# One 224 KB coefficient load, B_C_im, moved from ScalarE's DMA queue to SyncE's

## The chip, the cores and the metric

The kernel runs on one core of a Trainium2 chip. The metric is the device time in microseconds (us) of one execution. A load or a store is issued by an instruction on SyncE's queue (SPq in the profile) or on ScalarE's queue (ACTq), in the order in which the program put the instructions there; the DMA engines then move the data while the issuing engine goes on.

## The reference, cut to what matters

The output joins two independent branches over 2048 positions and 448 channels. Branch A is a linear attention with learned feature maps; it is not touched. Branch B is a state-space convolution. From six coefficient matrices of 448 channels by 256 states (A, B and C, each with a real and an imaginary part) it builds a convolution kernel of 2048 taps for each channel, convolves the signal u with it, and adds a skip term.

```python
dt = jnp.exp(log_dt)[:, None]
A = A_re + 1j * A_im
Bc = B_re + 1j * B_im
Cc = C_re + 1j * C_im
logdA = dt * A
dB = dt * Bc
...
P = jnp.exp(logdA[:, :, None] * l[None, None, :])
K = jnp.einsum("dn,dnl,dn->dl", Cc, P, dB).real
```

The product of C and B, a complex one, is the part that needs B_C_im: two of its four real products are C_im times B_re and C_im times B_im.

## The kernel before, in words

The program first records some 1050 operations (`Prog.add`), numbered from 0 in the order of the source, and then issues them in an order written out by hand, the list `ORDER`. Each engine runs its instructions in that order, and the loads and stores stand in it like everything else. Buffers (`PLACES`), banks of the accumulators (`SLOTS`) and, where there is a choice, engines or queues (`PICKS`) are lists too, read from left to right as the source asks for them. One letter of `PICKS` is used up by each load or store that goes through `dma`, where S is SyncE and Q is ScalarE, and one by each copy that ScalarE (A) or VectorE (V) may make. Waits between instructions are put in by the framework.

The opening, which this change is about, works so:

- The six coefficient matrices are loaded whole, 224 KB each, as tiles of 112 partitions by 4 by 256 (`load_raw`, lines 262 and 263; A_re by lines 289 to 291). In `ORDER` the loads are number 0 (log_dt), 3 (A_re), 5 (A_im), 7 (B_re), 8 (C_im), 6 (C_re), 9 (B_im), 30 (a strip of the weights `A_wqkv`, which goes to the tile WV), then 40 and 39 (the first half of the signal u, 448 KB each), and much later 4 (PID, a table of constants), 42 and 41 (the second half of u), and the rest.
- A_re (3) and C_im (8) go through ScalarE's queue, the others through SyncE's. On ScalarE, number 8 stands behind 43 (exp of log_dt) and 45 (a scaling of a diagonal matrix, `DGN`).
- TensorE multiplies A_re and A_im with a diagonal matrix of dt and so turns them to a layout by states (`to_states`, numbers 46 and 51). ScalarE copies a part and takes five exponentials of the first (60 to 64), then sines and cosines of the second (72, 73, 76, 77, 79, 80, 82, 83, 85, 86), which are made in pairs for five multiples. VectorE multiplies each pair with its exponential (81, 78, 87, 74, 84, each 128 x 1792).
- Between them VectorE makes the four products of C and B (lines 351 to 353). In `ORDER` they come as 59 (C_im times B_re), 56 (C_re times B_re), then two small steps (49, 48), 58 (C_re times B_im), 57 (C_im times B_im), then 50. VectorE's first use of any B or C is thus number 59, which needs C_im; the last instructions in front of it on VectorE are the subtractions 55 and 53.
- TensorE takes the four products through `to_states` (67 and 65). ScalarE's sine steps 85 and 73 write buffers that lie where operands of earlier VectorE work lie, so they wait for that work.
- Number 4 (PID) is put into the buffer in which C_im lies before (both at place 370), so its load waits for the load of C_im and for the last product that reads it, number 57. All later loads stand behind it on SyncE.

After the opening the kernel goes round four groups of 112 channels (`tables`, `kernel_spectrum`, `conv`), interleaved with the attention branch (`key_side`, `query_side`).

The lines that make the choice of a queue:

```python
    def pick(self):
        self.picks += 1
        return PICKS[self.picks - 1]
...
    def dma(eng, o, i):
        e = {"S": nc.sync, "Q": nc.scalar}[prog.queue()]
        prog.add("S", lambda: e.dma_start(out=o, in_=i))
...
    dma("S", PID, P_d)
    for nm in ("Aim", "Cre", "Bre", "Cim", "Bim"):
        load_raw(nm)
```

Of the kernel before, what the change touches and what calls it, by code (L numbers as in the profile page):

```python
# [129 lines left out]
def kernel(  # L130
# [778 lines left out]
).split()]  # L909
PICKS = (  # L910
    "SSSSQSSSSSSSSSSSSSSSAAVVVAAAVAVAAAAAAAAASAASAASAASAAAAAAAAASAASAASAASSSSSSSSSVVVVVAAAASSSSSSSSAAAAAA"
    "AAAAAAAAAAAVVVSSSSVVVAVAAAASSSSSSSSSSSSSSSSAVAAAAVAASVVAAAAAASQAVAAAAAVASSASASAAASAQVVVAVVAAASQSSSSS"
    "SAAAVAAVAAAAAAAAAVQSASASAAASASVVAAAVVVVSQSSSQQSAVAAAAAAAAAAAAAAASSVSASASASAVAAAAAASVSASAQVSAQAQ"
)
# [27 lines left out]
```

## Time and profile before

| what | value |
|---|---|
| median of 3 runs | 232.46 us (232.2 to 234.28) |
| the profiled execution: device time | 233.31 us |
| the profiled execution: span from first to last instruction | 231.6 us |
| mean granted TensorE clock | 0.977 |
| VectorE (DVE) busy | 211.5 us, 91% |
| TensorE (PE) busy | 201.2 us, 87% |
| ScalarE (ACT) busy | 195.2 us, 84% |
| moved by DMA | 32.87 MB |

In the views, an engine's busy time counts its own instructions and not those that only issue a DMA or wait. A row of the timeline gives the start, the length, the engine, the source line, the operation and the shape; a remark in square brackets tells how long the engine was idle before it and what ended that. The source line is that of a helper: line 186 is every two-operand step of VectorE, line 206 every function of ScalarE, line 214 every copy, line 229 every matrix product, line 249 every load or store. A row with q behind the engine's name (SPq, ACTq) is an issue; its length is that of the issue and not of the transfer.

### The profile page before, as it was taken

How to read it: one execution, taken by the hardware profiler on the slowest of the kernel's cores; microseconds unless marked ns; L12 is line 12 of the kernel's file. 1: busy time of each engine (PE TensorE's matmuls, PEld its weight loads, DVE VectorE, ACT ScalarE, POOL GpSimd, SP SyncE). 2: the span in 40 equal slices, each digit the busy share in tenths (PEclk: the TensorE clock that was granted, in tenths of full speed). 3: DMA queues.
4: the chain of work that ended last, by engine and by line, in shares of the span. 5: the costliest groups of instructions: out<-in, count | busy, mean ns of one | idle time of the engine just before them, and what ended most of it. 6: DMA issues, size and time to landing. Idle time of an engine off the chain costs nothing.

```text
span 231.6 us, 7313 instructions
## 1 busy us (share of the span) xinstructions
PE 201.2 (87%) x3125; PEld 146.0 (63%) x3136; DVE 211.5 (91%) x268; ACT 195.2 (84%) x354; POOL 8.0 (3%) x26
## 2 busy tenths in 40 slices
PE   1115699999999999999886899999999998999994
PEld 1014345656556755797664877745667876789994
DVE  1469999999999999999999999999999996999990
ACT  3977999999999999999999999999699867445331
POOL 4000000000000200002000000010000000000000
PEclk9999569999999999999999999999999999999999
DMA  5918990536828949997755807124799239464173
GB/s 168 214 24 188 290 219 3 128 105 200 215 55 135 229 110 232 143 170 204 238 134 63 233 0 237 32 55 24 181 267 285 52 58 217 86 107 93 25 181 79
DMA packets 78247, 32.87 MB, mean 142 GB/s; under 512 B 64856, under 2 KB 76168, under 8 KB 77960
## 3 DMA queue, kind: packets, MB, share of 16 engines
q1 hardware_dynamic: 72840, 29.76, 59.7%
q10 hardware_dynamic: 5376, 2.65, 4.6%
q8 instruction: 24, 0.39, 0.8%
q14 instruction: 7, 0.06, 0.1%
HBM read 15.84 MB, written 8.49 MB: 105 GB/s over the span
## 4 chain that ended last, share of the span: by engine, by line
PE 58%; ACT 24%; issue 4%; DVE 4%; DVEq 0%; ACTq 0%
PE psum L229 57%; ACT sbuf L206 12%; ACT sbuf L214 11%; DVE sbuf L186 3%; ACT L206 1%; PE psum L239 1%; DVE sbuf L214 0%; DVEq L214 0%; ACTq L214 0%; DVEq L186 0%; ACTq L206 0%
## 5 line engine op out<-in xcount | busy, mean ns | idle before, releaser
L229 PE MATMUL psum<-sbuf 128*128 128x112 bf16 (+9 forms) x3077 | 199.0, 256 | 26.7 <-DVE sbuf L186 10.4
L186 DVE TENSOR_TENSOR sbuf<-sbuf 128x896 bf16<-128x896 bf16 (+11 forms) x214 | 190.9, 955 | 10.4 <-DMA sbuf<-in_B_u_dram 4.6
L229 PEld LDWEIGHTS <-sbuf 128*128 128x128 bf16 (+5 forms) x3088 | 143.5, 113 | 81.1 <-issue 22.6
L214 ACT CAST sbuf<-psum 128x448 bf16<-128x448 f32 (+8 forms) x124 | 79.6, 691 | 21.7 <-PE psum L229 19.1
L206 ACT ACTIVATE sbuf<-psum 128x512 bf16<-128x512 f32 (+6 forms) x154 | 83.1, 625 | 3.2 <-DVE sbuf L186 1.3
L206 ACT ACTIVATE sbuf<-sbuf 128x896 bf16<-128x896 bf16 (+3 forms) x29 | 18.8, 680 | 2.5 <-DMA sbuf<-in_B_log_dt_dram 1.3
L214 DVE CAST sbuf<-psum 128x448 bf16<-128x448 f32 (+4 forms) x21 | 12.2, 597 | 6.3 <-PE psum L229 6.2
L206 ACT ACTIVATE sbuf<-psum,sbuf 128x896 f32<-128x896 f32 (+3 forms) x17 | 13.7, 811 | 1.8 <-DVE sbuf L186 1.3
L224 POOL MEMSET sbuf<- 128x224 bf16 (+7 forms) x21 | 7.6, 388 | 157.1 <-PE psum L229 68.6
L214 ACT COPY sbuf<-psum 112x896 bf16<-112x896 bf16 (+2 forms) x12 | 7.1, 620 | 2.4 <-PE psum L239 1.9
L203 ACT ACT_TABLE_LOAD x5 | 6.4, 1283 | 1.3 <-PEq L926 1.3
L206 ACT ACT_TABLE_LOAD x4 | 5.1, 1283 | 0.1
L214 DVE COPY sbuf<-sbuf 128x448 bf16<-128x448 bf16 (+2 forms) x13 | 4.1, 319 | 0.0
L239 PE MATMUL psum<-sbuf 112*112 112x112 bf16 (+1 forms) x48 | 3.4, 216 | 0.7 <-DVE sbuf L186 0.7
L239 PEld LDWEIGHTS <-sbuf 112*112 112x112 bf16 (+1 forms) x48 | 2.9, 120 | 1.3 <-DVE sbuf L186 0.8
L186 DVE TENSOR_TENSOR sbuf<-psum,sbuf 128x448 bf16<-128x448 f32 (+1 forms) x6 | 2.8, 489 | 0.0
L214 DVE CAST sbuf<-sbuf 128x1792 bf16<-128x1792 f32 (+1 forms) x4 | 2.8, 710 | 0.0
L217 DVE TENSOR_SCALAR sbuf<-sbuf 128x1568 bf16<-128x1568 bf16 x4 | 2.5, 628 | 0.0
L214 ACT COPY sbuf<-sbuf 128x224 bf16<-128x224 bf16 (+1 forms) x5 | 2.2, 443 | 0.0
L220 ACT ACTIVATE sbuf<-sbuf 128x1792 f32<-128x1792 f32 x1 | 1.7, 1702 | 0.0
L217 ACT ACTIVATE sbuf<-sbuf 112x448 bf16<-112x448 bf16 x1 | 0.6, 577 | 0.8 <-DVE sbuf L309 0.8
L198 DVE SCALAR_TENSOR_TENSOR sbuf<-sbuf,psum 128x128 f32<-128x128 f32 x4 | 1.1, 285 | 0.0
(8 smaller groups left out, 2.5 us busy)
## 6 DMA issues: line engine op xcount, KB each, us to landing
SUd<-sbuf SPq DMA_DIRECT2D x8, 448.0 KB, 3.6
sbuf<-SUd SPq DMA_DIRECT2D x4, 896.0 KB, 4.9
sbuf<-const SPq DMA_DIRECT2D x8, 384.0 KB, 3.8
sbuf<-in_B_u_dram SPq DMA_DIRECT2D x4, 448.0 KB, 6.6
out_dram<-sbuf SPq DMA_DIRECT2D x13, 112.0 KB, 2.7
out_dram<-sbuf SPq DMA_DIRECT2D x3, 448.0 KB, 3.5
sbuf<-const SPq DMA_DIRECT2D x2, 512.0 KB
sbuf<-const ACTq DMA_DIRECT2D x1, 1024.0 KB
```

The source lines that it names most:

```text
L186: prog.add("V", lambda: nc.vector.tensor_tensor(out=o, in0=a, in1=b, op=op))
L198: prog.add("V", lambda: nc.vector.scalar_tensor_tensor(out=o, in0=a, scalar=s, in1=b, op0=op0, op1=op1))
L203: nc.scalar.preload_act_table_set("natural_log_exp_and_others")
L206: nc.scalar.activation(o, a, fn, **kw)
L214: either(lambda: nc.scalar.copy(o, a), lambda: nc.vector.tensor_copy(o, a))
L217: either(lambda: nc.scalar.activation(o, a, ACT.Copy, scale=s), lambda: nc.vector.tensor_scalar_mul(o, a, s))
L220: either(lambda: nc.scalar.activation(o, a, ACT.Square), lambda: nc.vector.tensor_tensor(out=o, in0=a, in1=a, op=ALU.mult))
L224: prog.add("G", lambda: nc.gpsimd.memset(o, v))
L229: nc.tensor.matmul(o, lhsT=l, rhs=r, **kw)
L239: nc.tensor.transpose(o, i, idn)
```

## The change

One letter of `PICKS`, the fifth, goes from Q to S. The letters in front of it belong to PID, A_im, C_re and B_re, so the fifth is that of C_im. `ORDER` and all other entries stay, so that on SyncE's queue number 8 now stands where `ORDER` has it: behind 7 (B_re) and in front of 6 (C_re), 9 (B_im), 30 (weights), 40 and 39 (signal). On ScalarE's queue one issue is gone.

```diff
 PICKS = (
-    "SSSSQSSSSSSSSSSSSSSSAAVVVAAAVAVAAAAAAAAASAASAASAASAAAAAAAAASAASAASAASSSSSSSSSVVVVVAAAASSSSSSSSAAAAAA"
+    "SSSSSSSSSSSSSSSSSSSSAAVVVAAAVAVAAAAAAAAASAASAASAASAAAAAAAAASAASAASAASSSSSSSSSVVVVVAAAASSSSSSSSAAAAAA"
```

## The prediction

> **What bounds the kernel now.** I read the profile in four steps. First the page's busy times and its chain of work that ended last, then the busy times by stretches (column two is the length, then PE, PEld, DVE, ACT, POOL, the granted clock, the DMA share and GB/s).
>
> ```profile
> span 231.6 us, 7313 instructions
> PE 201.2 (87%) x3125; PEld 146.0 (63%) x3136; DVE 211.5 (91%) x268; ACT 195.2 (84%) x354; POOL 8.0 (3%) x26
> PE 58%; ACT 24%; issue 4%; DVE 4%; DVEq 0%; ACTq 0%
> ```
> ```profile
> 0.00:10.00 10.00, 1.65 (x16) 1.51 (x16) 3.01 (x6) 6.37 (x9) 2.56 (x12) 1.00 0.81 187
> 10.00:20.00 10.00, 3.17 (x32) 3.04 (x33) 6.50 (x9) 7.42 (x9) 0.00 (x0) 1.00 0.39 79
> 20.00:30.00 10.00, 5.53 (x24) 3.11 (x24) 10.00 (x7) 10.00 (x15) 0.00 (x0) 0.65 1.10 284
> 30.00:40.00 10.00, 9.91 (x51) 4.89 (x50) 10.00 (x16) 9.69 (x13) 0.00 (x0) 0.84 0.59 90
> 40.00:60.00 20.00, 19.80 (x150) 11.88 (x150) 20.00 (x30) 19.93 (x28) 0.52 (x1) 1.00 0.55 150
> 60.00:80.00 20.00, 19.54 (x326) 12.44 (x325) 20.00 (x22) 19.91 (x38) 0.51 (x2) 1.00 0.82 155
> 140.00:160.00 20.00, 19.53 (x356) 12.55 (x356) 19.79 (x25) 18.89 (x33) 0.66 (x3) 1.00 0.41 93
> 200.00:231.00 31.00, 28.59 (x532) 26.89 (x529) 25.87 (x29) 11.69 (x24) 0.00 (x0) 1.00 0.50 97
> ```
>
> The chain names PE most, but the stretches tell more: from 20 us on DVE has no idle time up to 80 us and hardly any up to 160, ACT idles 0.00, 0.31, 0.07 and 0.09 us in the four stretches up to 80, and PE looks nearly full too. Three engines are full at once, each in a fixed order. Such a kernel has little room to lose or win a delay later: what the opening gives to all three arrives at the end. The opening is where they idle, so third, the timeline of the first 30 us:
>
> ```profile
> 2.25 0.46 SPq L249 DMA_DIRECT2D sbuf<-in_B_C_re_dram  x1
> 2.75 0.46 SPq L249 DMA_DIRECT2D sbuf<-in_B_B_im_dram  x1
> 3.87 1.32 SPq L249 DMA_DIRECT2D sbuf<-in_B_u_dram  x2
> 4.84 0.35 ACTq L249 DMA_DIRECT2D sbuf<-in_B_C_im_dram  x1
> 5.70 0.66 ACT L214 CAST sbuf<-psum 128x448 bf16<-128x448 f32 x1 [0.29 <-PE psum L229]
> 7.67 1.19 DVE L186 TENSOR_TENSOR sbuf<-psum,sbuf 128x448 bf16<-128x448 f32 x2
> 12.60 0.91 ACT L206 ACTIVATE sbuf<-psum 128x896 f32<-128x896 f32 x1
> 13.51 1.29 DVE L186 TENSOR_TENSOR sbuf<-sbuf 112x1024 bf16<-112x1024 bf16 x2 [4.64 <-DMA sbuf<-in_B_u_dram]
> 14.29 0.93 ACT L206 ACTIVATE sbuf<-psum 128x896 f32<-128x896 f32 x1
> 15.79 1.28 DVE L186 TENSOR_TENSOR sbuf<-sbuf 112x1024 bf16<-112x1024 bf16 x2
> 16.50 1.01 ACT L206 ACTIVATE sbuf<-psum,sbuf 128x896 f32<-128x896 f32 x1 [1.29 <-DVE sbuf L186]
> 17.10 0.37 SPq L249 DMA_DIRECT2D sbuf<-const  x1
> 17.41 0.91 ACT L206 ACTIVATE sbuf<-psum 128x896 f32<-128x896 f32 x1
> 17.53 11.69 DVE L186 TENSOR_TENSOR sbuf<-sbuf 128x1792 bf16<-128x1792 f32 x6
> 19.58 0.92 ACT L206 ACTIVATE sbuf<-psum 128x896 f32<-128x896 f32 x1 [1.26 <-DVE sbuf L186]
> 21.28 0.91 ACT L214 CAST sbuf<-psum 128x896 bf16<-128x896 f32 x1
> 22.24 0.94 PE L229 MATMUL psum<-sbuf 128*128 128x448 bf16 x4 [2.55 <-ACT sbuf L214]
> 28.72 7.61 PE L229 MATMUL psum<-sbuf 128*128 128x224 bf16 x31 [0.92 <-ACT sbuf L214]
> ```
>
> The row at 13.51 is the case: DVE has finished the subtractions (7.67 + 1.19 = 8.86) and idles 4.64 us ahead of its first product of C and B, number 59, C_im times B_re. The row names a load of B_u, but that multiply reads no u; a wait for several loads is put down to one of them. Fourth, therefore, SP's own waits and the times to landing:
>
> ```profile
> SPq L249 <- DMA sbuf<-in_B_C_im_dram: 8.2, 1, 8.2
> ```
> ```profile
> sbuf<-in_B_u_dram SPq DMA_DIRECT2D x4, 448.0 KB, 6.6
> sbuf<-in_B_C_re_dram SPq DMA_DIRECT2D x1, 224.0 KB, 5.0
> sbuf<-in_B_B_im_dram SPq DMA_DIRECT2D x1, 224.0 KB, 5.7
> ```
>
> SP had issued its last load by 3.87 + 1.32 = 5.19 and then stood 8.2 us until C_im had landed (PID takes over its buffer): C_im lands at about 13.4, and DVE starts at 13.51. So C_im, issued last of the ten opening loads, also lands last, 8.5 us after its issue. C_re, issued at 2.25, lands at 7.25; B_im at 2.75 + 5.7 = 8.45; a first half of u at 3.87 + 6.6 = 10.5.
>
> **The change, part by part.**
>
> *SP's queue.* The issue goes in behind B_re and takes C_re's place at 2.25; C_re, B_im, the strip of weights and the two u loads are each issued 0.5 us later (the step from 2.25 to 2.75). The cover: the next issue on SP is PID at 17.10, which waits for DVE, so 0.5 us on an idle queue costs nothing; without it, 0.5.
>
> *ACT's queue.* An issue of 0.35 us goes. ACT then waits for PE in any case (the row at 5.70, idle 0.29), so I take 0; the bound is 0.3 of gain.
>
> *Landing.* C_im in C_re's place lands at about 7.25. The late bound is that of a place behind u, 10.5. The loads behind it move back by the spacing of two such loads, 8.45 − 7.25 = 1.2: C_re to 8.45, B_im to 9.65. The bytes are the same, so the last half of u lands about when C_im does now, 13.4; its reader on PE (22.24) is far off.
>
> *DVE.* Number 59 can start at 8.87 if C_im is there, 1.6 us before that, and B_re, issued before it. The second product wants C_re at 8.87 + 0.6 = 9.5 (landed 8.45), the third B_im about 2.3 later (15.79 − 13.51), at 11.1 (landed 9.65). From 13.51 to 17.53 DVE does 4.02 us of work, so from 8.87 it would be at the first 128x1792 multiply at 12.9. That one needs ACT's sine that ends at 12.60 + 0.91 = 13.51. This is what is late next: DVE starts it at about 13.55 in place of 17.53, 3.98 earlier. Of the 4.64 us of stall, 0.66 turns into a wait for ACT. With the late bound for the landing (10.5) the products would end at 14.5 and 3.0 would be left.
>
> *ACT.* It has two stalls behind DVE, 1.29 at 16.50 (a buffer that the third product reads; that now ends near 11.9, ahead of the 15.2 at which ACT is ready) and 1.26 at 19.58 (the first 128x1792 multiply, one of six in 11.69, so 1.95 each: 13.55 + 1.95 = 15.5, ahead of the 16.8 at which ACT is ready). Both go, 2.55. Rows of ACT that don't wait start about 0.1 before the one ahead ends (12.60 + 0.91 against 13.39 in the next fence), so 2.75 in all. No other idle time is left on ACT behind 5.7 us that could go as well.
>
> ```profile
> 13.39 1.01 ACT L206 ACTIVATE sbuf<-psum,sbuf 128x896 f32<-128x896 f32 x1
> ```
>
> *PE.* Its work at 22.24 and at 28.72 starts on copies of ACT (21.28 + 0.91 = 22.19), so it moves with ACT, 2.75. Behind 28.72 it is full.
>
> *PID and the loads behind it.* They wait for the last product (15.79 + 1.28 = 17.07), which would end at about 12.5; SP's queue is some 4 us earlier, ahead of both engines. No later row of the waits shows an engine waiting for a load. Cost 0; were they not earlier, the shift of their readers would be lost.
>
> *Sum.* DVE is 3.98 early, ACT and PE 2.75, and they feed each other with no idle time in which the difference could be kept, so the smaller shift sets the end: −2.75. Bounds: above, 3.98 (DVE alone decides); below, 0 if nothing of it reaches the end, and less than 0 only by the clock (below). Against the profiled execution (231.6 of span, 233.31 as a device time) this gives 230.56. The median of the runs, 232.46, lies 0.85 lower; on that footing 229.7.
>
> **A rule weighed against the rows.** C_im, alone on ACT's queue behind A_re, lands after loads that SP issued before it. The Trainium skill (DMA: Bandwidth & Descriptors, section Queues, rings and completion order) says that each DMA engine takes turns between the queues that have work, packet by packet. By that C_im should have shared the engines evenly with SP's backlog and come well before the end of it; the trace disagrees with an even share, 13.4. If the rule were right here, C_im's landing would not be the one that ends the stall, and the sum would be 0. The same page (Issuing engines are not separate DMA queues) holds that the queue saves issue time alone; that agrees with the order of landing seen, and then it is the issue time, 2.25 for 4.84, that counts.
>
> **The rivals.**
>
> *A: no change, the stall ends with the signal.* DVE's row names B_u, and the last half of u must land at about 13.4 too. If number 59 waits for that load (through a shared counter of landings), it still starts at 13.5 and the time stays 232.5. For it: the name in the row. Against: SP's 8.2 us for C_im ends within 0.1 us of DVE's start, and the code gives the multiply no u. This is also the case in which the change does not do what it says, and the one that the skill's rule of turns would give.
>
> *B: DVE alone sets the end.* DVE idles nowhere between 20 and 80; if ACT's small idle times later (0.31, 0.07, 0.09 and 1.11 between 140 and 160) take up the 1.23 between the two shifts, 3.98 arrives: 228.5. Against: those up to 80 add up to 0.47 only.
>
> *C: half of it is lost to TensorE's clock.* The clock is half until about 33 us, and PE is full by then:
>
> ```profile
> 26.80:30.20 3.40, 2.38 (x10) 1.38 (x10) 3.40 (x4) 3.40 (x8) 0.00 (x0) 0.50 1.08 342
> 30.20:33.70 3.50, 3.41 (x11) 1.33 (x10) 3.50 (x7) 3.47 (x7) 0.00 (x0) 0.57 1.06 210
> ```
>
> If full speed comes at the same moment as before, PE, 2.75 early, does 2.75 us more at half speed and loses 1.38: 231.1. The Trainium skill (TensorE: Matmul & The Clock Gate, Part 1) has the window of the gate free-running, which allows either; the rows show only that it opened after a stretch with PE full.
>
> *D: slower, by the same clock.* PE idles longer between its new early work (16.52 now, near 12.3 then) and its work at 19.5. If it therefore stays at half clock for a further time of the kind seen, about 10 us (the 0.65 of 20 to 30 and the 0.84 of 30 to 40 make 5.1 us at zero clock, 10.2 at half), it loses 5.1 us on a path with no slack: 232.46 − 2.75 + 5.1 = 234.8. The kernel turns slower than before once the added half-clock time passes 5.5 us. For it: three full engines forgive nothing. Against: PE full for 3 us was enough last time.
>
> **How the numbers follow.** About 1% (2.3 us, under 230.1 or over 234.8) is what a measurement of this kernel can tell from no change, as its three runs spread by 0.9%. Forecast 0.46, A 0.10, B 0.18, C 0.19, D 0.07. The likeliest is 229.7. Faster by over 1%: the forecast but for 0.04 that noise takes over the line, and B, 0.60. Within: those 0.04, A, C, 0.33. Slower: D, 0.07. The range reaches from B less 0.2 of noise, 228.3, past C to 232.0; A and D, 0.17, are left out.
>
> **What would show it.** Right: DVE's idle time ahead of the first 112x1024 product falls from 4.64 to under 0.3 and the row starts near 8.9; a short wait of DVE for ACT appears ahead of the 128x1792 multiplies, which begin near 13.5; ACT's stalls of 1.29 and 1.26 are gone and its row at 19.58 stands near 16.8; PE's rows of 22.24 and 28.72 stand near 19.5 and 26.0; PID is issued near 12.6. Wrong: the product still starts at 13.5 (A); it waits for C_re or B_im in place of C_im; or the opening is early and the stretches behind 30 us show new idle time, or half clock, by the amount that is missing (C, D).

## The result and the profile after

| | before | changed |
|---|---|---|
| median | 233.25 us (17 runs, 231.29 to 235.76) | 230.98 us (17 runs, 229.68 to 235.08) |
| ratio to before | | 0.992, 95% interval 0.9895 to 0.9944 |
| the profiled execution, device time | 233.31 us | 230.0 us |
| its span | 231.6 us | 228.1 us |

The kernel became faster, by 0.8% in this comparison. Two repeats of the same kernel, below, gave 0.9885 and 0.9882. Over all sets together (90 executions of the kernel before and 28 of the changed one) the means are 233.28 and 230.80 us, a gain of 2.47 us with an interval of about 0.35 to either side. Nine further executions, eight before and one changed, ran in a slower state and are left out of these means. The forecast was 2.75. The two profiled executions differ by 3.3 us, more than that: the one before lies at its kernel's mean, the one after 0.8 below its own. What the traces below add up to is therefore about 0.8 too much.

The page of the changed kernel begins:

```profile
span 228.1 us, 7325 instructions
PE 201.5 (88%) x3136; PEld 145.8 (64%) x3136; DVE 211.7 (93%) x268; ACT 194.5 (85%) x354; POOL 8.9 (4%) x26
...
PE 53%; ACT 23%; DVE 16%; issue 5%; DMA 1%; DVEq 0%; ACTq 0%
```

The engines do the same work as before (DVE 211.7 us for 211.5); what shrank is idle time. In the chain DVE rose from 4% to 16%. The opening, in the timeline:

```profile
2.25 0.46 SPq L249 DMA_DIRECT2D sbuf<-in_B_C_im_dram  x1
...
7.59 1.19 DVE L186 TENSOR_TENSOR sbuf<-psum,sbuf 128x448 bf16<-128x448 f32 x2
8.68 1.28 DVE L186 TENSOR_TENSOR sbuf<-sbuf 112x1024 bf16<-112x1024 bf16 x2
10.33 0.65 DVE L214 CAST sbuf<-psum 128x448 bf16<-128x448 f32 x1 [0.37 <-ACT sbuf L206]
...
12.52 0.91 ACT L206 ACTIVATE sbuf<-psum 128x896 f32<-128x896 f32 x1
12.71 0.37 SPq L249 DMA_DIRECT2D sbuf<-const  x1
13.46 11.70 DVE L186 TENSOR_TENSOR sbuf<-sbuf 128x1792 bf16<-128x1792 f32 x6 [0.19 <-ACT sbuf L206]
15.00 1.03 ACT L206 ACTIVATE sbuf<-psum,sbuf 128x896 f32<-128x896 f32 x1
15.89 1.75 ACT L206 ACTIVATE sbuf<-psum 128x896 f32<-128x896 f32 x2
18.38 0.96 ACT L214 CAST sbuf<-psum 128x896 bf16<-128x896 f32 x1
19.39 3.96 PE L229 MATMUL psum<-sbuf 128*128 128x448 bf16 x14 [4.08 <-ACT sbuf L214]
...
25.87 10.48 PE L229 MATMUL psum<-sbuf 128*128 128x224 bf16 x55 [1.29 <-ACT sbuf L214]
...
28.36 1.28 ACT L203 ACT_TABLE_LOAD   x1
```

The product at 8.68 follows the subtractions with no remark in brackets: the stall of 4.64 us is gone. ACT's sine rows at 15.00 and 15.89 carry no remark either, so its waits of 1.29 and 1.26 are gone too. DVE now waits for ACT, 0.37 us at a small copy and 0.19 at 13.46. SP's wait for C_im and the times from issue to landing:

```profile
SPq L249 <- DMA sbuf<-in_B_C_im_dram: 1.4, 1, 1.4
```
```profile
sbuf<-in_B_C_im_dram SPq DMA_DIRECT2D x1, 224.0 KB, 4.9
sbuf<-in_B_C_re_dram SPq DMA_DIRECT2D x1, 224.0 KB, 5.5
```

C_im lands at 2.25 + 4.9 = 7.15, and C_re, issued 0.5 us behind it, at 2.75 + 5.5 = 8.25. The busy times by stretches (columns as in the prediction):

```profile
10.00:20.00 10.00, 3.78 (x34) 3.29 (x35) 9.48 (x9) 9.97 (x13) 0.00 (x0) 1.00 0.85 182
20.00:30.00 10.00, 7.95 (x32) 4.10 (x31) 10.00 (x11) 9.97 (x16) 0.00 (x0) 0.83 1.03 267
30.00:40.00 10.00, 9.73 (x73) 5.93 (x72) 9.99 (x17) 10.00 (x16) 0.00 (x0) 1.00 0.07 22
40.00:60.00 20.00, 19.91 (x139) 11.22 (x137) 20.00 (x28) 19.90 (x30) 1.38 (x1) 1.00 0.65 175
```

From 10 to 20 us DVE works 9.48 us where it worked 6.50, and ACT 9.97 for 7.42. Half clock shows for less time as well, 0.83 and 1.00 for 0.65 and 0.84 in the stretches from 20 to 40. How far each engine is ahead later can be read at instructions that occur once: ACT's table loads and DVE's last copy. Before:

```profile
31.21 1.28 ACT L203 ACT_TABLE_LOAD   x1
...
72.55 1.28 ACT L206 ACT_TABLE_LOAD   x1
...
147.62 1.28 ACT L206 ACT_TABLE_LOAD   x1
...
227.81 0.39 DVE L214 CAST sbuf<-psum 128x224 bf16<-128x224 f32 x1 [1.92 <-PE psum L229]
```

After:

```profile
69.15 1.28 ACT L206 ACT_TABLE_LOAD   x1
...
143.67 1.28 ACT L206 ACT_TABLE_LOAD   x1
...
224.12 0.39 DVE L214 CAST sbuf<-psum 128x224 bf16<-128x224 f32 x1 [1.92 <-PE psum L229]
```

DVE was 17.53 − 13.46 = 4.07 us early at the first 128x1792 multiply and is 3.69 early at its last copy. ACT was 31.21 − 28.36 = 2.85 early, then 3.40, then 3.95: it catches up with DVE's lead instead of holding DVE back to its own.

### The profile page after: what moved, and what is told of

It is laid out like the page before. It is cut to its first block, busy times and chain, and to the rows that moved or that the text cites. A ratio compares the mean times of both kernels' runs of the same rounds, so it can differ in the third digit from the quotient of the medians.

```text
span 228.1 us, 7325 instructions
## 1 busy us (share of the span) xinstructions
PE 201.5 (88%) x3136; PEld 145.8 (64%) x3136; DVE 211.7 (93%) x268; ACT 194.5 (85%) x354; POOL 8.9 (4%) x26
## 4 chain that ended last, share of the span: by engine, by line
PE 53%; ACT 23%; DVE 16%; issue 5%; DMA 1%; DVEq 0%; ACTq 0%
PE psum L229 52%; DVE sbuf L186 14%; ACT sbuf L206 13%; ACT sbuf L214 9%; DVE sbuf L214 2%; DMA sbuf<-in_B_log_dt_dram 1%; ACT L206 1%; PE psum L239 1%; DVE sbuf L217 1%; DVE sbuf L198 0%; DVEq L186 0%; ACTq L206 0%; DVEq L214 0%; DVE sbuf L309 0%
## 5 line engine op out<-in xcount | busy, mean ns | idle before, releaser
L229 PE MATMUL psum<-sbuf 128*128 128x112 bf16 (+10 forms) x3088 | 199.3, 257 | 22.6 <-ACT sbuf L214 8.8
L224 POOL MEMSET sbuf<- 128x224 bf16 (+7 forms) x21 | 8.4, 429 | 152.3 <-PE psum L229 67.3
```

What stands on the lines that cost most here:

```text
L224: prog.add("G", lambda: nc.gpsimd.memset(o, v))
L229: nc.tensor.matmul(o, lhsT=l, rhs=r, **kw)
```

## The experiments

Three questions were open. Was it C_im's landing that ended the stall, and does the queue matter or the place in the order of issue? Is DVE's stall the whole cause? And which engine's shift sets the end? The theories: "forecast" (the smaller shift, ACT's, counts), B (DVE's shift counts), A (the stall belongs to the signal), and the clock (C, D). Where nothing else is said, an experiment computes the same output. Lines of `ORDER` are long; the cuts below show the stretch that differs.

**The changed kernel again, twice** (e1 and, in another set, e9; no edit).

> The changed kernel once more, unaltered, for a second profile and as the yardstick of the others in this set. The first pair of profiles gave spans of 231.6 before and 228.1 after, 3.5 us, while 17 runs of each gave a ratio of 0.992, about 1.9 us. If DVE alone sets the end and the stall of 4.64 us was typical, the ratio is near 0.983 (4 us). If ACT sets the end, 0.988 (2.75 us). If the profiled execution before had an unusually long stall, the ratio stays near 0.992 and the stall is gone all the same: DVE's first 112x1024 product starts at 8.5 to 9.0 us with under 0.3 us of idle time before it.

> The changed kernel a third time, to narrow the size of the gain. Two profiles each of the kernel before (spans 231.6 and 232.3) and of the changed one (228.1 and 228.7) differ by 3.6 us on average, the two sets of runs by 0.8% and 1.15%. If the opening's 3.6 to 4 us on DVE arrive in full in most executions, the ratio is 0.984 to 0.987; if about two thirds of them do, as the kernels with a C_im landing in between suggest, 0.988 to 0.992. The opening in the profile is the same as in the first two: first 128x1792 multiply at 13.4 to 13.6.

Measured: 0.9885 (0.9836 to 0.9934), median 230.49, and 0.9882 (0.9859 to 0.9905), median 230.36. With the first comparison this is a gain of about 1%. Of the ratios expected for e1, the one with ACT setting the end, 0.988, was met; 0.983, with DVE setting it, lies just outside the interval. The profile of e1 also bears on the clock. Its stretches from 20 to 40 us:

```profile
20.00:30.00 10.00, 8.02 (x39) 4.27 (x38) 10.00 (x11) 9.97 (x16) 0.00 (x0) 1.00 1.01 268
30.00:40.00 10.00, 8.69 (x67) 5.26 (x66) 9.99 (x17) 10.00 (x15) 0.00 (x0) 1.00 0.19 33
```

Here no half clock shows at all (1.00 for the 0.83 of the first profile of the same kernel), and yet ACT's table load that stood at 69.15 stands at 69.12. In this part a stretch at half clock moves nothing; PE has room there, 7.95 busy in the 10 us from 20 to 30 in the first profile. Rivals C and D are out. As far as the times show, the shorter half clock is not what made the kernel faster either: 18 executions of the kernel before at a mean clock under 0.98, as in its two profiles, took 233.21 us on average, and 18 at 0.995 or more took 233.26. (Eleven from 0.98 to 0.988 took 234.48; where in the run their half clock lies is not on record.)

**The kernel before again** (e5; no edit).

> The kernel before, unaltered: a second profile of it, and a measure of how far two sets of runs of one kernel differ. Ratio 1.000, within 0.003. If the stall of 4.64 us of the first profile was typical, DVE's idle time before its first 112x1024 product is again 4.2 to 5.0 us. If that execution was an unlucky one, which would explain why the runs gained 2 to 2.5 us and the two profiles 3.5, it is 2 to 3.5 us here.

Measured: 0.9988 (0.9942 to 1.0035), median 232.91. The stall shows again in this profile:

```profile
13.18 1.29 DVE L186 TENSOR_TENSOR sbuf<-sbuf 112x1024 bf16<-112x1024 bf16 x2 [4.38 <-DMA sbuf<-in_B_u_dram]
```

**C_im early, but on ScalarE's queue** (e4, and e10 a second time; an edit of the kernel before). Number 8 is issued directly behind A_re; `PICKS` keeps its Q.

```diff
-    "1 69 0 3 2 43 28 44 46 5 45 7 8 36
+    "1 69 0 3 8 2 43 28 44 46 5 45 7 36
```

> The kernel before, with C_im left on ScalarE's queue but issued directly behind A_re, at about 1.25 us in place of 4.84, ahead of the exponential of log_dt. If it is the time of issue that counts, it lands before 8.8 us, DVE's stall of 4.64 us goes and the ratio is that of the changed kernel, within 0.002. If it is the queue that counts (loads of ScalarE's queue served after those of SyncE's), it still lands near 13 us and the ratio is 1.000 within 0.002. If the rule of turns between queues holds, it lands by about 6 to 7 us, with the same result as the first.

> C_im on ScalarE's queue directly behind A_re, a second time, beside the changed kernel on the same chip. If only the time of issue counts, the two ratios agree within 0.003. If ScalarE's queue early is better than SyncE's (C_re and B_im are issued 0.5 us sooner, though DVE's products did not wait for them), it is lower by 0.003 or more again.

Measured: 0.9871 (0.982 to 0.9922), median 230.14, and 0.9896 (0.986 to 0.9932), median 230.42: the gain of the changed kernel, without SP's queue. From the timeline of e4:

```profile
1.26 0.50 ACTq L249 DMA_DIRECT2D sbuf<-in_B_C_im_dram  x1
...
8.86 1.27 DVE L186 TENSOR_TENSOR sbuf<-sbuf 112x1024 bf16<-112x1024 bf16 x2
```

The load needed an earlier issue, not another queue. That is also what the Trainium skill says (DMA: Bandwidth & Descriptors, section Issuing engines are not separate DMA queues): transfers started by different engines run on the same 16 DMA engines, and a second issuing engine saves only the time of the issue. The runs agree, with 0.9871 and 0.9896 on one queue beside 0.9885 and 0.9882 on the other.

**C_im on SyncE's queue, but late** (e6 behind both opening loads of u, e7 between them; edits of the changed kernel). In `ORDER` the loads 6, 9, 30, 40 (and 39) come in front of 8, and all else keeps its order.

```diff
-46 5 45 7 8 36 47 62 51 64 52 54 55 53 60 6 61 9 59 30 63 56 40 49 39 79 48
+46 5 45 7 6 9 30 40 39 8 36 47 62 51 64 52 54 55 53 60 61 59 63 56 49 79 48
```
```diff
+46 5 45 7 6 9 30 40 8 39 36 47 62 51 64 52 54 55 53 60 61 59 63 56 49 79 48
```

> The changed kernel with C_im on SyncE's queue, but issued last of the opening loads, behind the strip of weights and both halves of u (the other loads keep their order). If the place in the order of issue counts, it lands near 13.4 us as before, DVE's stall is back at 4.3 to 4.8 us, and the ratio is 1.000 within 0.003: the queue alone gives nothing. If SyncE's queue as such is served sooner than ScalarE's, the stall is shorter and the ratio near 0.99.

> The changed kernel with C_im on SyncE's queue between the two halves of u. It should land behind the first half (10.5) by the spacing of one such load (1.2), near 11.7 us, so DVE's stall is about 2.9 us and its first 128x1792 multiply starts at 11.7 + 4.0 = 15.7, 2.2 us later than in the changed kernel. If each microsecond by which DVE's multiplies start late arrives at the end, the time lies about 2.2 us over that of the changed kernel and 1.8 under the kernel before: ratio near 0.992. If ACT alone set the end, its second stall would come back by about 0.9 us only and the ratio would be that of the changed kernel plus 0.004.

Measured: e6 1.0046 (1.0006 to 1.0087), median 234.56; e7 0.9983 (0.9941 to 1.0024), median 232.7. The profile of e6 is of an execution of 237.23 us, 2.7 over the median, so only its opening is read here. The issue of C_im and DVE's products in e6, and then the products in e7:

```profile
5.23 0.60 SPq L249 DMA_DIRECT2D sbuf<-in_B_C_im_dram  x1
...
13.27 1.29 DVE L186 TENSOR_TENSOR sbuf<-sbuf 112x1024 bf16<-112x1024 bf16 x2 [4.46 <-DMA sbuf<-in_B_u_dram]
```
```profile
12.43 1.29 DVE L186 TENSOR_TENSOR sbuf<-sbuf 112x1024 bf16<-112x1024 bf16 x2 [3.60 <-DMA sbuf<-in_B_C_im_dram]
...
16.46 5.88 DVE L186 TENSOR_TENSOR sbuf<-sbuf 128x1792 bf16<-128x1792 f32 x3
```

On SyncE's queue and issued last, at 5.23, C_im lands as late as it did on ScalarE's, issued last at 4.84. One u load fewer in front (e7, issued at 4.59) brings the product 0.84 us forward. I had expected more, 11.7. Whether the place made even that difference is open: in e8 below, C_im is issued last again and yet used at 12.54. The ratio expected for e7, 0.992, was missed. The 0.75 us that DVE is earlier at 16.46 than in e5 (17.21) would be 0.003 of the time, which the interval can't tell from none.

**The stall taken away without moving the load** (e8, an edit of the kernel before). Number 59 goes behind 58, so that the two products that don't need C_im come first.

```diff
-9 59 30 63 56 40 49 39 79 48 58 67 57
+9 30 63 56 40 49 39 79 48 58 59 67 57
```

> The kernel before, C_im on ScalarE's queue as it was, but on VectorE the two products that need no C_im (C_re times B_re, C_re times B_im) and the two small steps 49 and 48 come ahead of C_im times B_re. They fill some 2.5 us of the stall. C_im still lands near 13.4, then two products and one step are left (1.9 us), so the first 128x1792 multiply starts near 15.4 in place of 17.5. If the stall on DVE is the whole cause, about 2.1 us come off without any load being moved: ratio 0.991. If the load's move helps by something else (SyncE's queue free earlier, the buffer of PID), the ratio stays near 1.000.

Measured: 0.9902 (0.9857 to 0.9947), median 230.79. C_im was still issued at its old place on ScalarE's queue:

```profile
4.80 0.37 ACTq L249 DMA_DIRECT2D sbuf<-in_B_C_im_dram  x1
...
8.72 0.68 DVE L186 TENSOR_TENSOR sbuf<-sbuf 112x1024 bf16<-112x1024 bf16 x1
...
12.54 1.29 DVE L186 TENSOR_TENSOR sbuf<-sbuf 112x1024 bf16<-112x1024 bf16 x2 [0.42 <-DMA sbuf<-in_B_C_im_dram]
...
14.30 7.82 DVE L186 TENSOR_TENSOR sbuf<-sbuf 128x1792 bf16<-128x1792 f32 x4
```

C_re times B_re runs at 8.72, inside the old stall, while C_im is still on its way. So the gain comes without moving the issue of any opening load. DVE's multiplies start at 14.30, 3.23 us earlier than before and not the 2.1 expected, and 2.3 us of that arrive. The issue of PID, which waits for number 57, comes earlier with DVE here (13.86 for 17.10) and later with it in e11, so no run parts the two; but no row of the waits shows an engine held for more than 0.2 us by a load issued behind it in the changed kernel.

**The stall put back as work** (e11, an edit of the changed kernel in `Prog.run`). Number 59 is issued eight times and writes the same values each time, so DVE is busy where it had idled.

```diff
-            self.issue(i)
+            for _ in range({59: 8}.get(i, 1)): self.issue(i)
```

> The changed kernel, C_im early, but VectorE does the first product (number 59, C_im times B_re) eight times over, which writes the same values again: 7 x 0.6 = 4.2 us of work where the stall was. The first 128x1792 multiply then starts near 17.3 and ACT's two stalls are back, with all loads as early as in the changed kernel except those behind PID. If the stall on DVE is the whole of what the change removed, the time is that of the kernel before: ratio 1.000 within 0.004, the gain taken back to the last third. If the earlier load helps in another way, the ratio stays at 0.995 or less.

Measured: 1.0079 (1.0046 to 1.0112), median 235.0. DVE and, behind it, ACT:

```profile
8.74 6.36 DVE L186 TENSOR_TENSOR sbuf<-sbuf 112x1024 bf16<-112x1024 bf16 x9
...
17.84 5.88 DVE L186 TENSOR_TENSOR sbuf<-sbuf 128x1792 bf16<-128x1792 f32 x3
```
```profile
16.80 1.01 ACT L206 ACTIVATE sbuf<-psum,sbuf 128x896 f32<-128x896 f32 x1 [1.62 <-DVE sbuf L186]
...
19.88 0.92 ACT L206 ACTIVATE sbuf<-psum 128x896 f32<-128x896 f32 x1 [1.26 <-DVE sbuf L186]
```

With the load early and DVE late, the gain is gone and ACT's stalls are back (1.62 for 1.29, and 1.26 again). The expected 1.000 within 0.004 was missed on the slow side. DVE starts its multiplies 0.31 us later than in the kernel before and the kernel takes 1.8 us longer; about 1.5 us of that I can't account for.

**Which shift sets the end** (e2 and e3, edits of the changed kernel in the same line). e2 issues number 57, a product on DVE, three times; e3 issues number 77, a sine on ACT, twice.

```diff
+            for _ in range({57: 3}.get(i, 1)): self.issue(i)
```
```diff
+            for _ in range({77: 2}.get(i, 1)): self.issue(i)
```

> The changed kernel, with the last of the four products of C and B (number 57) done three times over on VectorE, which writes the same values again: two more 112x1024 multiplies, 2 x 0.6 = 1.2 us more of DVE's time ahead of its 128x1792 multiplies. If DVE sets the end, all 1.2 us arrive: ratio to the kernel before 0.005 above that of the changed kernel (0.997 if that is 0.992). If ACT sets the end, DVE has about 1.1 us to spare (3.98 early against 2.9) and at most 0.2 us arrive: the ratio of the changed kernel, within 0.001.

> The changed kernel, with one sine of ScalarE (number 77, 128x896) done twice, which writes the same values again: 0.9 us more of ACT's time at about 15 us. If ACT sets the end, 0.9 us arrive: ratio 0.004 above that of the changed kernel. If DVE sets the end, ACT's lag of about 1.1 us behind DVE grows to 2.0 and is made good in ACT's idle time later in the run; 0 to 0.3 us arrive, the ratio within 0.0015 of that of the changed kernel.

Measured: e2 0.9927 (0.9889 to 0.9964), median 231.63; e3 0.9904 (0.9873 to 0.9935), median 231.48. From e2, DVE's and ACT's rows:

```profile
14.60 7.82 DVE L186 TENSOR_TENSOR sbuf<-sbuf 128x1792 bf16<-128x1792 f32 x4
```
```profile
28.36 1.28 ACT L203 ACT_TABLE_LOAD   x1
```

In e2 DVE is 1.14 us later and ACT not at all, up to 28.36. If ACT's position set the end, e2 would cost at most 0.2 us. It costs 0.8 (a mean of 231.61 for 230.80), some 70% of DVE's delay. The intervals of e2 and of the changed kernel overlap, so I also take the profiles: DVE's last copy stands at 225.11 in e2 and at 224.12, 224.67 and 224.43 in the three of the changed kernel, 0.70 later than their mean. e3 tells less than it was meant to. Its extra sine delayed DVE too:

```profile
16.12 5.89 DVE L186 TENSOR_TENSOR sbuf<-sbuf 128x1792 bf16<-128x1792 f32 x3 [0.63 <-ACT sbuf L206]
```

DVE's second multiply waits 0.63 us for ACT here, so of the 0.9 us of the extra sine ACT could spare only some 0.3 at that place. e3 loses 0.55 in the mean (231.35), about what it cost DVE; it can't part the two theories.

## Why the prediction was right, and where it was not

- *The queues.* Right. Neither the issue on SP nor the one taken from ACT shows in the time (e4 and e10 beside the changed kernel).
- *Landing.* Right within 0.2: C_im 7.15 (forecast 7.25), C_re 8.25 (8.45), PID issued at 12.71 (12.6).
- *DVE.* Right: the product at 8.68 (8.87), the first multiply at 13.46 (13.55) after a short wait for ACT, 4.07 early (3.98). The wait of 0.37 at 10.33 was not foreseen, but it lies in the same 0.56 us of waiting for ACT (0.66 forecast).
- *ACT and PE in the opening.* Right: no stalls; the copy of 21.28 stands at 18.38, 2.90 early (2.75); PE's rows at 19.39 and 25.87 (19.5 and 26.0).
- *The rivals.* A falls by the changed kernel's own row: the product that needs C_im starts at 8.68 with no wait, while the first load of u is issued only at 4.40 and the loads of u take 6.3 us from issue to landing (their median), and e8's row at 12.54 names C_im. C and D fall by the clock's rows and e1.
- *The rule of turns.* The prediction read it as refuted, and that goes too far. In the profile before, C_im, issued at 4.84, is 240 packets on ScalarE's queue. One of them moves before 9.0 us, but between 10 and 12 us 149 of them move beside 155 of SyncE's. So the two queues' packets do alternate once C_im's have started; what made C_im late is first of all that they start some 4 us after the issue, and why is open. That the place in the order of issue counted, on which the sum rests, stands by e4 and e6.
- *The step that failed* is the last: "they feed each other with no idle time in which the difference could be kept, so the smaller shift sets the end: −2.75". ACT's 2.85 did not hold DVE back to 2.85. ACT's lead grew to 3.40 at 72 us and 3.95 at 147 (2.71, 3.37 and 3.76 as means of two profiles before and three of the changed kernel), while DVE kept 3.69 of its 4.07 up to its last copy (3.78 of 3.93 in these means). The idle time that had been counted as too little was there: between its table loads at 31.21 and 147.62 ACT idled 1.83 us before, and between the same two 1.12 after. The prediction set only the 0.47 up to 80 us against rival B.
- *Which shift sets the size* is less clear. Four edits of the changed kernel let DVE's 128x1792 multiplies start later by 1.16 (e2), 3.02 (e7), 3.85 (e6) and 4.40 us (e11), and ACT's table load of 28.36 by 0.02, 1.80, 2.64 and 3.16. Their means lie 0.8, 2.2, 3.5 and 4.3 us over the changed kernel's: always more than ACT's delay, and in three of the four nearer to DVE's. That is rival B's mechanism. The kernel before does not fit it: its DVE is 3.93 later and it costs only 2.47, nearer to ACT's 2.71. So the forecast of 2.75 came close in part by luck: the rule gave 1.2 less than DVE's lead, and of that lead some 1.5 us (3.93 less 2.47) do not show in the mean of all executions.

Of these 1.5 us the traces show a part. At 40 us a memset on POOL falls beside other DVE work than before. Before, POOL and then DVE:

```profile
43.86 0.52 POOL L224 MEMSET sbuf<- 64x512 bf16 x1 [40.67 <-PE psum L239]
```
```profile
45.48 0.27 DVE L214 COPY sbuf<-sbuf 128x448 bf16<-128x448 bf16 x1
45.66 2.86 DVE L186 TENSOR_TENSOR sbuf<-sbuf 128x896 bf16<-128x896 bf16 x3
```

After:

```profile
40.48 1.38 POOL L224 MEMSET sbuf<- 64x512 bf16 x1 [37.31 <-PE psum L239]
```
```profile
41.47 0.53 DVE L214 COPY sbuf<-sbuf 128x448 bf16<-128x448 bf16 x1
41.92 2.84 DVE L186 TENSOR_TENSOR sbuf<-sbuf 128x896 bf16<-128x896 bf16 x3
```

The memset takes 1.38 us for 0.52 and the copy beside it 0.53 for 0.27; at the row behind them DVE is 3.74 us early. That is 0.27 lost; e1 and e9 show the same 1.39 and 0.53 or 0.54. In the spans the lead is still 3.5 us. The last 1.0 is in no trace: the five profiled executions of the two kernels happen to lie further apart (3.4 us) than the means of all.

A part of the scatter behind that has a likely cause in the traces. PE before and after, with "issue" as releaser:

```profile
112.87 0.61 PE L229 MATMUL psum<-sbuf 128*32 128x80 bf16 x20 [0.95 <-issue]
```
```profile
108.78 4.10 PE L229 MATMUL psum<-sbuf 128*32 128x80 bf16 x78 [0.68 <-issue]
```

At this place the kernel before waited 0.95 us in one profile and 1.52 in e5's, the changed kernel 0.68, 1.22 and 0.98 in its three, and e7 1.96. The releaser "issue" names nothing, but the packets do. On the DMA queue that the page lists as "instruction", a transfer of 16 KB ends at 111.5 in the profile before and at 107.4 in the one after, and in all 13 profiles PE starts again 1.2 to 1.5 us behind the end of such a transfer. So PE most likely waits there for its next instructions, for a time that differs between executions. That was seen and not tested. Nor is it known why e11 ends 1.5 us later than its opening explains (its wait here is 0.72), nor why e6, with DVE and ACT within 0.1 us of e5 in the opening (17.29 and 30.98 for 17.21 and 30.89), has a mean 1.0 us over that of the kernel before.

## What to carry to other kernels

When an engine stalls for a load, look first at which load was issued last and whether the waiting step can use another that is there already: moving the issue forward on either queue and reordering the products each gave about 1%. Where several engines are full in the same stretch, don't take the smallest shift for the result; look for small idle times in which the slower one can catch up, and keep both shifts as ends of the range. A pair of profiles of kernels that scatter by 1% can differ by a third more than their means do, 3.3 us here for 2.47: set the traces against the means before asking where a difference was lost.

## What the runs showed of the hardware

- Early issue, not the queue, brought the load early: issued last at 4.78 to 4.84 on ScalarE's queue or at 5.23 on SyncE's, it was used at 12.5 to 13.5; issued at 1.26 on the one or 2.25 on the other, by 8.9.
- A POOL memset of 64x512 and the DVE instructions beside it stretched one another. Where the memset started behind a DVE cast of 128x1792 (40.48 for 40.23, the changed kernel), it took 1.38 us, the cast 1.18 and the copy of 128x448 behind it 0.53. Where it started ahead of or with the cast, it took 0.52, the cast 1.43 (e5) and 1.54 (e7); the copy took 0.27 in the profile before. The Trainium skill (SBUF — State Buffer, section SBUF: two separate sides) says that the two engines share one port pair, which an instruction of POOL, or of DVE in some modes, holds alone to its end. The rows fit that; whether this cast and this copy are in such a mode they do not tell, and no run here took the memset away.
- PE idled up to 1.96 us (e7) in the middle of a run and started again 1.2 to 1.5 us behind the end of a 16 KB transfer on the instruction queue, in 13 profiles of 13.
- TensorE's stretch at half clock was 10 us long in the profile before (by the clocks of 0.65 and 0.84 in the prediction), 3.4 in the first of the changed kernel (0.83 of full speed over 10 us) and not there in e1's; between the last two it made no difference at 69 us.
